# Two units' queries, and two units' keys, in one transfer each, with the keys' odd chunks in front

## The chip, the cores and the metric

One core of a Trainium2 chip runs the whole program. The metric is the device time of one execution in microseconds (us); a kernel's figure is the median over its runs. The core has five engines with an instruction queue each: TensorE (PE, matmuls; its weight loads are listed as PEld), VectorE (DVE), ScalarE (ACT), GpSimd (POOL) and SyncE (SP), which here only issues DMA transfers and waits for semaphores. Each queue runs in order.

## The reference, cut to what matters

```
scores = 0.125 * q @ k^T                      # 4 batches, 8 heads, 576 positions, 64 wide
heads 0..3: a query sees itself and the 31 keys before it
heads 4..7: a query sees keys at distance 0, 4, 8, ... below 128
attn = softmax(scores);  x = attn @ v         # x: 2304 tokens x 512
logits = x @ phi                              # soft mixture of experts, 8 experts x 4 slots
slot_input = softmax over tokens(logits)^T @ x
slot_out[e] = relu(slot_input[e] @ w1[e]) @ w2[e]
x = softmax over slots(logits) @ slot_out
h = x @ w_in;  g = max(h, 0) + alpha * min(h, 0);  out = g @ w_out
```

All arrays are float32. For heads 4 to 7 the host sorts positions by their remainder modulo 4, so that a dilated window becomes a plain one of 32.

## The kernel before

**Units and groups.** A unit u (16 of them) is one batch and two heads; with head width 64 its q and k fill 128 partitions, 576 columns each. A unit is cut into 9 blocks of 64 queries, and 8 consecutive blocks over the units make a group g (18 of them), so a group touches one or two units. Per group PE preloads the mask (`sm`, L254), computes the scores (`s`, L263: 16 matmuls of 64 keys), later transposes the probabilities (`t`, L298) and multiplies with v (`pv`, L311). DVE and ACT do the softmax between them (`max`, `sub`, `exp`, `sum`, `rec`), POOL the normalising, ACT the copies out of PSUM (`te`, and half of `ev`). Between the groups PE also computes the router's logits (`lt`), transposes of x (`x`) and the slot sums (`part`).

**How q, k and v come in.** For each unit SP issues one transfer for q, one for k (`load_qk`, L240, 288 KB each, 2304 bytes a partition) and one for v (`load_v`, L248, 576 KB, 4608 bytes a partition). q lands in a raw buffer: that of units 2 and 3 lies in `xs_m`, all others use two in `q_m` in turn. ACT and DVE then copy it, one head each (`emit_qx`, tasks `qx`), into one of four slots with zeros between the heads. k has four slots of 32 + 576 columns (the 32 are zeros, for the block before the first), v has four. So q of unit u waits for the `qx` of unit u - 2, k for the last `s` of unit u - 4, `qx` for that too, v for the last `pv` of unit u - 4.

**The expert weights** come in 32 transfers of 1024 KB (8192 bytes a partition, L185) on the same SP queue, in the order of use. Twelve have buffers of their own, which are free from the start; nine go into the memory of q, k, v, the probabilities and xs when attention has left it; the last eleven reuse buffers as experts consume them. Then follow the first 1024 KB transfers of the last layer (`w_f`, L183).

**The order** on every engine in the attention part is made at build time by a planner (`schedule`): a list of tasks with their needs, a due time (`k - 20` for q and k) and a cost of occupation and latency (`COST`). It takes the task that could start first; SP is one of its engines ("dma"), and a weight transfer is what it takes when nothing of attention may start. The chip then runs each engine's queue in that order and waits on semaphores.

**After attention** come the slot sums, then the experts (`emit_l1` L596, `emit_hT` L609, `emit_l2` L618) with some matmuls without use (`warm`, L407) around the last expert, then the conversion of the first `w_f` (`conv`, L668 to L678) and the last layer, which takes the rest of the time and doesn't touch q, k or v.

## Time and profile before

| what | us |
|---|---|
| median of 3 runs (387.76 to 390.1) | 389.87 |
| the profiled execution | 390.64 |
| its span, first to last instruction | 388.9 |
| PE busy in the span | 364.7 |
| attention, up to the first expert matmul | 97.3 |
| experts, up to the last L618 | 141.5 |
| the last layer | the rest |

The profiled execution is 1.7 us longer than its span, and 0.8 us above the median. 75.19 MB move in all, most of it in the first 150 us; over the whole span that is 193 GB/s. A profile says busy time by engine, but the three stages have different limits, so each is read from its own stretch.

### The profile page before, as it was taken

The numbers are of one execution on the slowest core, as the hardware profiler recorded it, in microseconds if no ns is written. First come the engines' busy times: TensorE is split into PE (matmuls) and PEld (weight loads), VectorE is DVE, ScalarE is ACT, GpSimd is POOL, SyncE is SP. The second block draws the span as 40 slices with busy tenths as digits, with TensorE's granted clock in tenths as the row PEclk, the third lists the DMA queues.
The fourth block names the chain that finished last, engine by engine and source line by source line (L and its number), as shares of the span: only waits on it lengthen the run. The fifth ranks groups of instructions, "written<-read, shape, count | busy, mean of one in ns | idle before, by whom it ended". The sixth has DMA issues, their size and how long they took to land.

```text
span 388.9 us, 7912 instructions
## 1 busy us (share of the span) xinstructions
PE 364.7 (94%) x3126; PEld 272.1 (70%) x3126; DVE 262.3 (67%) x454; ACT 218.2 (56%) x467; POOL 142.4 (37%) x125
## 2 busy tenths in 40 slices
PE   7689899998999688899999999999999999999995
PEld 4477687865444256577877787887788878778884
DVE  5888889765166139989999998939974324234363
ACT  2478778664232028877766746656754645446460
POOL 4223222220000004446456556545564444444460
PEclk9999999999999899989999999999999999999998
DMA  8999999999999995053332325100000000001336
GB/s 294 393 353 360 397 397 407 408 418 422 420 419 421 420 421 201 10 207 109 109 110 108 108 110 163 55 0 0 3 1 0 2 0 1 2 0 56 108 128 197
DMA packets 17173, 75.19 MB, mean 193 GB/s; under 512 B 2128, under 2 KB 2528, under 8 KB 10992
## 3 DMA queue, kind: packets, MB, share of 16 engines
q1 hardware_dynamic: 16160, 72.98, 48.9%
q10 hardware_dynamic: 912, 1.64, 1.2%
q8 instruction: 24, 0.39, 0.4%
q14 instruction: 13, 0.11, 0.1%
q0 software_dynamic: 64, 0.07, 0.1%
HBM read 69.97 MB, written 4.72 MB: 192 GB/s over the span
## 4 chain that ended last, share of the span: by engine, by line
PE 50%; DVE 22%; DMA 16%; ACT 6%; issue 3%; POOL 1%; SPq 1%; DVEq 0%; POOLq 0%; ACTq 0%
PE y L802 32%; DMA w<-w 9%; DMA q_m<-qk 7%; DVE gs L796 5%; PE pv L311 3%; DVE wo_lo L685 3%; PE hb L788 2%; PE si L391 2%; DVE pt_m L675 2%; PE x L382 2%; DVE pt_m L678 2%; PE s L263 2%; DVE e_m L672 2%; DVE e_m L675 2%; DVE e_m L670 1%
## 5 line engine op out<-in xcount | busy, mean ns | idle before, releaser
L896 POOL TENSOR_TENSOR gls<-gs,ghs 128x384 fp32r<-128x384 f32 x96 | 117.6, 1241 | 170.4 <-ACT ghs L327 142.0
L802 PE MATMUL y<-wo_hi,ghs 128*128 128x512 f32 x289 | 97.6, 401 | 0.8 <-ACT ghs L327 0.4
L796 DVE SCALAR_TENSOR_TENSOR gs<-gs,beta_s,hb 128x384 f32<-128x384 f32 x96 | 56.5, 609 | 51.6 <-ACT gs L890 49.2
L802 PE MATMUL y<-wo_lo,ghs 128*128 128x512 f32 x289 | 89.3, 394 | 0.0
L802 PE MATMUL y<-wo_hi,gls 128*128 128x512 f32 x289 | 86.2, 394 | 2.3 <-POOL gls L896 2.3
L890 ACT ACTIVATE gs<-hb 128x384 f32<-128x384 f32 x96 | 44.9, 492 | 36.8 <-PE hb L788 31.4
L327 ACT CAST ghs<-gs 128x384 fp32r<-128x384 f32 x96 | 49.4, 517 | 28.0 <-DVE gs L796 27.5
L802 PEld LDWEIGHTS y<-wo_hi,gls 128*128 128x128 f32 x289 | 54.4, 189 | 14.3 <-POOL gls L896 3.6
L802 PEld LDWEIGHTS y<-wo_hi,ghs 128*128 128x128 f32 x289 | 53.7, 189 | 14.9 <-issue 1.8
L802 PEld LDWEIGHTS y<-wo_lo,ghs 128*128 128x128 f32 x289 | 54.4, 189 | 10.7 <-issue 0.2
L293 POOL TENSOR_TENSOR e_m<-e_m,l 128x512 f32<-128x512 f32 x18 | 19.1, 1062 | 58.9 <-DVE l L289 36.4
L788 PE MATMUL hb<-cpack,mpack 128*128 128x384 f32 x96 | 31.5, 346 | 1.4 <-DVE mpack L782 0.8
L263 PEld LDWEIGHTS s<-q_m 128*64 128x64 f32 x576 | 18.7, 138 | 7.5 <-issue 4.5
L311 PE MATMUL pv<-pt_m,v_m 128*64 128x64 f32 x576 | 20.0, 224 | 2.8 <-ACT pt_m L327 2.7
L311 PEld LDWEIGHTS pv<-pt_m,v_m 128*64 128x64 f32 x576 | 18.1, 138 | 6.3 <-ACT pt_m L327 3.8
L263 PE MATMUL s<-q_m 128*64 128x64 f32 x576 | 21.2, 225 | 1.1 <-ACT q_m L327 1.0
L788 PEld LDWEIGHTS hb<-cpack,mpack 128*128 128x128 f32 x96 | 17.8, 188 | 5.7 <-DVE mpack L782 1.5
L327 ACT COPY pt_m<-t 64x512 f32<-64x512 f32 x36 | 20.8, 579 | 0.9 <-PE t L298 0.2
L670 DVE TENSOR_SCALAR pt_m<-pt_m 128x1024 f32<-128x1024 f32 (+1 forms) x9 | 8.1, 900 | 18.9 <-ACT pt_m L668 18.9
L599 ACT ACTIVATE v_m<-h,rinv 128x256 f32<-128x256 f32 x8 | 3.8, 474 | 20.8 <-PE h L596 16.2
L329 DVE COPY xt<-pv 128x256 f32<-128x256 f32 (+7 forms) x32 | 9.5, 306 | 8.7 <-ACT xt L327 8.5
L618 PE MATMUL o<-w,hT 128*32 128x512 f32 x88 | 12.5, 640 | 3.1 <-DMA w<-w 3.1
(157 smaller groups left out, 492.6 us busy)
## 6 DMA issues: line engine op xcount, KB each, us to landing
w<-w SPq DMA_DIRECT2D x23, 1024.0 KB, 12.8
v_m<-v SPq DMA_DIRECT2D x16, 576.0 KB, 7.0
q_m<-qk SPq DMA_DIRECT2D x30, 288.0 KB, 6.0
q_m<-w_f SPq DMA_DIRECT2D x8, 1024.0 KB, 5.0
v_m<-w_f SPq DMA_DIRECT2D x7, 1024.0 KB, 4.8
q_m<-w SPq DMA_DIRECT2D x4, 1024.0 KB, 17.7
v_m<-w SPq DMA_DIRECT2D x2, 1024.0 KB, 16.7
e_m<-w SPq DMA_DIRECT2D x1, 1024.0 KB, 15.0
```

What stands on the lines that cost most here:

```text
L263: mm(s[r:r + 64, col:col + 64], lhsT=q_of(u)[:, 2 * o:2 * o + 64], rhs=k_of(u)[:, o:o + 64], start=False, stop=True, skip_group_check=True)
L293: nc.gpsimd.tensor_tensor(out=e, in0=e, in1=bc(e_[g, "l"], 128, 8, 64), op=ALU.mult)
L311: mm(pv[hs, n], lhsT=vv[u % 4][:, c, hs], rhs=pts[:, NBS * (g % 2) + n, h], start=True, stop=True, skip_group_check=True)
L327: nc.scalar.copy(out=out, in_=in_)
L618: mm(o[32 * g:32 * g + 32, :], lhsT=ht[:, 4 * r + g, 28 - 4 * e:60 - 4 * e], rhs=w[:, g, :], start=(e == 0 and r == 0), stop=(e == NE - 1 ...
L670: nc.vector.tensor_scalar(out=t, in0=t, scalar1=2.0 ** -15, scalar2=FMAX, op0=ALU.max, op1=ALU.min)
L675: nc.vector.scalar_tensor_tensor(out=ti, in0=w[:, 1::2], scalar=-0x40000000, in1=ti, op0=ALU.bitwise_and, op1=ALU.bitwise_or)
L788: mm(hb[i], lhsT=mpack[:, 128 * f:128 * f + 128], rhs=cpack[:, t0:t0 + 384], start=True, stop=True)
L796: nc.vector.scalar_tensor_tensor(out=g, in0=g, scalar=beta_s[:, f:f + 1], in1=hb[i], op0=ALU.mult, op1=ALU.add)
L802: mm(y[steps[s][0], t][:, sl], lhsT=g, rhs=wo_hl[p == 1][:, f, sl], start=start, stop=stop, skip_group_check=True)
L890: lambda s=s, i=i: nc.scalar.activation(out=half(gs, s, i, 4), in_=hb[i], func=AF.Relu, scale=-1.0),
L896: lambda s=s, i=i: nc.gpsimd.tensor_tensor(out=half(gls, s, i, 6), in0=half(gs, s, i, 4), in1=half(ghs, s, i, 6).bitcast(F32), op=ALU.subt ...
```

## The change

Units are taken in pairs. For units 0 and 1 q and k come as before, one transfer per unit and array. For the 14 other units one transfer brings both units' q (576 KB, 4608 bytes a partition) and one both units' k. The raw q of a pair lies in `xs_m` for units 2 and 3, and in one buffer in `q_m` for all others. k has two slots of pairs, with one stretch of 32 zeros in front of each instead of one per unit. The order of a unit's 18 chunks of 32 keys is changed on the host: the nine odd ones first, then the nine even ones. The 64 keys of a score matmul are then two runs of 32 columns, 288 or 320 columns apart, and for the second half of a block the odd chunk comes first; mask and v (built on the host) follow that order. The number of matmuls, copies and softmax instructions stays.

A pair's q now waits for the `qx` of both units of the pair before it (for units 4 and 5: of 0 and 1), its k for the last `s` of both units two pairs before. The planner makes a new order of all attention tasks from that and from the new costs. The diff also has a way to copy parts of v on POOL (`COPIED`), which is empty here and makes no instruction. The one-element constant of ones becomes a column, set before the first matmul instead of later.

```
-            q=(0.75, 2.9), k=(0.75, 2.9), ...
+            q=(0.75, 2.9), k=(0.75, 2.9), qq=(1.45, 3.6), ...
+COPIED = ()
-KZ = S + WIN
+KP = 2 * S + WIN
...
-            j = 64 * c + kj - 32 * (1 - x)
+            j = 64 * c + (kj + 32) % 64 if x else 64 * c + kj - 32
...
+    def k_pair(p):
+        return part(q_m[:, NQ * QZ:], p % 2, KP)
+
+    def keys(u, c, x):
+
+        a, n = NQ * QZ + KP * (u // 2 % 2) + S * (u % 2) + 32 * (c + x), S // 2 + 32 * (1 - x)
+        return q_m[:, a:a + 2 * n].rearrange("p (b k) -> p b k", b=2)[:, :, 0:32]
+
+    def q_pair(p):
+        return xs_m[:, 0:2 * S] if p == 1 else q_m[:, NQ * QZ + 2 * KP:][:, 0:2 * S]
+
     def q_raw(u):
-        return part(xs_m, u - 2, S) if u in (2, 3) else part(q_m[:, NQ * (QZ + KZ):], u % 2, S)
+        return part(q_pair(u // 2), u % 2, S)

-    def load_qk(u, x):
-        nc.sync.dma_start(out=k_of(u)[:, WIN:] if x else q_raw(u), in_=qk[u, :, x])
+    def load_qk(p, x, c0=0, c1=2 * S):
+        nc.sync.dma_start(out=(k_pair(p)[:, WIN:] if x else q_pair(p))[:, c0:c1], in_=qk[p, :, x, c0:c1])
...
-                    mm(s[r:r + 64, col:col + 64], lhsT=q_of(u)[:, 2 * o:2 * o + 64], rhs=k_of(u)[:, o:o + 64],
+                    mm(s[r:r + 64, col:col + 64], lhsT=q_of(u)[:, 2 * o:2 * o + 64], rhs=keys(u, c, x),
...
+                p, odd = divmod(u, 2)
+                if first[u] == g and p == 0:
+                    task(("q", u), "dma", lambda u=u: load_qk(0, 0, S * u, S * u + S), [], k - 20)
+                    task(("k", u), "dma", lambda u=u: load_qk(0, 1, S * u, S * u + S), [], k - 20)
+                elif first[u] == g and not odd:
+                    task(("q", u), "dma", lambda p=p: load_qk(p, 0), [("qx", w, h) for w in {1: (), 2: (0, 1)}.get(p, (u - 2, u - 1)) for h in range(2)],
+                         k - 20, "qq")
+                    task(("k", u), "dma", lambda p=p: load_qk(p, 1), [("s", last[u + 1 - NQ])] if u >= NQ else [], k - 20, "qq")
                 if first[u] == g:
-                    task(("q", u), "dma", lambda u=u: load_qk(u, 0), [("qx", {4: 0, 5: 1}.get(u, u - 2), h) for h in range(2) if u > 3], k - 20)
-                    task(("k", u), "dma", lambda u=u: load_qk(u, 1), [("s", last[u - NQ])] if u >= NQ else [], k - 20)
...
+        nc.vector.memset(ones_s, 1.0)
         zero = pt_m[:, 0:512]
...
+        for i in range(2):
+            nc.vector.memset(k_pair(i)[:, 0:WIN], 0.0)
         for i in range(NQ):
-            nc.vector.memset(k_of(i)[:, 0:WIN], 0.0)
...
-        nc.vector.memset(one_s, 1.0)
```

SP's queue, from the first transfer after units 0 and 1 to the first expert weight. `xs_m` and `q_m` from `qk` are q or k, `v_m` is v, `w` an expert weight; the number at the end of a row is a repeat. Before:

```order
L240 DMA xs_m<-qk 128x576
L240 DMA q_m<-qk 128x576
L248 DMA v_m<-v 128x1152
L240 DMA xs_m<-qk 128x576
L240 DMA q_m<-qk 128x576
L248 DMA v_m<-v 128x1152
L240 DMA q_m<-qk 128x576 x2
L248 DMA v_m<-v 128x1152
L240 DMA q_m<-qk 128x576 x2
L248 DMA v_m<-v 128x1152
L240 DMA q_m<-qk 128x576 x4
L185 DMA w_80<-w 128x2048
```

The same stretch of the change, and two pairs further:

```order
L250 DMA xs_m<-qk 128x1152
L250 DMA q_m<-qk 128x1152
L259 DMA v_m<-v 128x1152 x2
L250 DMA q_m<-qk 128x1152 x2
L259 DMA v_m<-v 128x1152 x2
L187 DMA w_80<-w 128x2048
L250 DMA q_m<-qk 128x1152 x2
L259 DMA v_m<-v 128x1152
L187 DMA w_81<-w 128x2048
L259 DMA v_m<-v 128x1152
L250 DMA q_m<-qk 128x1152
```

The first weight now stands in front of q and k of units 6 and 7, where it stood behind them; the second stands in front of those of units 8 and 9.

PE's queue around the scores of group 6, which are the first to need unit 6 (the third `s` row from here on is group 7's; `t`, `pv` and `lt` are named above). Before:

```order
L298 MATMUL t<-eye_s,e_m 128x128 x4
L254 LDWEIGHTS m_m
L254 MATMUL s<-m_m 128x512
L263 MATMUL s<-q_m 64x64 x16
L341 MATMUL lt<-xt_116,phi_s 32x192 x3
L298 MATMUL t<-eye_s,e_m 128x128 x4
L311 MATMUL pv<-pt_m,v_m 64x64 x16
L254 LDWEIGHTS m_m
L254 MATMUL s<-m_m 128x512
L263 MATMUL s<-q_m 64x64 x16
L311 MATMUL pv<-pt_m,v_m 64x64 x16
```

The same stretch of the change:

```order
L317 MATMUL t<-eye_s,e_m 128x128 x4
L273 LDWEIGHTS m_m
L273 MATMUL s<-m_m 128x512
L360 MATMUL lt<-xt_116,phi_s 32x192 x3
L317 MATMUL t<-eye_s,e_m 128x128 x4
L330 MATMUL pv<-pt_m,v_m 64x64 x16
L282 MATMUL s<-q_m 64x64 x16
L317 MATMUL t<-eye_s,e_m 128x128 x4
L273 LDWEIGHTS m_m
L273 MATMUL s<-m_m 128x512
L330 MATMUL pv<-pt_m,v_m 64x64 x16
L282 MATMUL s<-q_m 64x64 x16
```

The scores of group 6 moved behind the logits, the transposes of group 3 and the `pv` of group 2, and one more group's transposes come before the scores of group 7.

## Rows read from the trace of the kernel before

**Rows 1.** The page's 40 slices: DMA busy in tenths, and GB/s.

```profile
DMA  8999999999999995053332325100000000001336
GB/s 294 393 353 360 397 397 407 408 418 422 420 419 421 420 421 201 10 207 109 109 110 108 108 110 163 55 0 0 3 1 0 2 0 1 2 0 56 108 128 197
```

**Rows 2.** Windows (stretch, length, busy by engine, clock, DMA share, GB/s).

```profile
5.00:10.00 5.00, 3.65 (x68) 2.33 (x66) 3.06 (x9) 3.02 (x4) 0.29 (x1) 1.00 1.04 398
10.00:15.00 5.00, 3.32 (x67) 2.56 (x68) 4.69 (x11) 2.05 (x4) 1.04 (x1) 1.00 1.05 402
...
25.00:30.00 5.00, 4.49 (x103) 3.38 (x100) 4.25 (x10) 4.56 (x9) 0.00 (x0) 1.00 0.93 322
...
120.00:125.00 5.00, 4.91 (x60) 2.22 (x59) 3.33 (x7) 1.82 (x5) 0.00 (x0) 1.00 1.01 418
```

**Rows 3.** Chain of waits, experts (start, us, what ran or was waited for).

```profile
97.33 1.09 PE h L596 x16
...
98.45 14.03 DMA w<-w
...
112.54 21.38 DMA w<-w
...
133.96 1.84 PE o L618 x8
135.79 2.38 PE st L407 x12
...
139.17 1.31 PE st L407 x10
140.48 1.04 PE o L618 x8
...
142.03 0.67 ACT pt_m L668
```

**Rows 4.** PE's timeline, last experts (start, us; idle before, and who ended it).

```profile
127.53 1.91 PE L596 MATMUL h<-w,slotT 128*32 128x256 f32 x32
131.56 1.07 PE L618 MATMUL o<-w,hT 128*32 128x512 f32 x8 [2.12 <-DMA w<-w]
132.55 0.44 PE L609 MATMUL t<-eye_s,v_m 128*128 128x128 f32 x2
133.96 1.84 PE L618 MATMUL o<-w,hT 128*32 128x512 f32 x8 [0.97 <-DMA w<-w]
```

**Rows 5.** SP's timeline: a steady stretch of 1024 KB transfers.

```profile
119.99 0.33 SPq L183 DMA_DIRECT2D q_m<-w_f  x1
122.48 0.33 SPq L183 DMA_DIRECT2D xs_m<-w_f  x1
```

**Rows 6.** Windows around the experts' end (clock is the third number from the right).

```profile
129.40:134.00 4.60, 1.51 (x18) 0.43 (x17) 0.00 (x0) 0.66 (x2) 0.00 (x0) 1.00 1.01 420
134.00:137.50 3.50, 3.50 (x16) 1.89 (x17) 0.00 (x0) 0.00 (x0) 0.00 (x0) 0.52 1.00 419
```

**Rows 7.** The page's DMA issues: KB each, median us from issue to landing.

```profile
v_m<-v SPq DMA_DIRECT2D x16, 576.0 KB, 7.0
q_m<-qk SPq DMA_DIRECT2D x30, 288.0 KB, 6.0
```

**Rows 8.** Chain of waits, first 41 us: landings of q that ACT waited for.

```profile
10.31 9.50 DMA q_m<-qk
...
19.89 0.67 ACT q_m L327
20.56 0.53 ACT e_m L280
...
35.33 5.04 DMA q_m<-qk
```

**Rows 9.** SP's timeline, where it waits for a copy of q.

```profile
12.44 0.33 SPq L248 DMA_DIRECT2D v_m<-v  x1
17.70 3.21 SPq L240 DMA_DIRECT2D q_m<-qk  x4
```

**Rows 10.** PE's timeline, groups 6 and 9.

```profile
24.40 1.15 PE L263 MATMUL s<-q_m 128*64 128x64 f32 x32
25.48 0.53 PE L341 MATMUL lt<-xt,phi_s 128*32 128x192 f32 x6
25.94 0.65 PE L298 MATMUL t<-eye_s,e_m 128*128 128x128 f32 x4
26.70 1.15 PE L311 MATMUL pv<-pt_m,v_m 128*64 128x64 f32 x32
...
35.70 1.15 PE L263 MATMUL s<-q_m 128*64 128x64 f32 x32
```

**Rows 11.** DVE's timeline: the zeros in front of k.

```profile
1.36 0.09 DVE L504 MEMSET q_m<- 128x32 f32 x1
```

More of the change, by code (lines that the diff above doesn't have):

```diff
@@ L159, in tile_kernel @@
     beta_s = const.tile([128, DFF // 128], F32, name="beta_s")
[L160 removed]
+    ones_s = const.tile([128, 1], F32, name="ones_s")
+    one_s = ones_s[0:1]
     slotT = keep.tile([128, 4, NS], F32, name="slotT")
@@ L247, in load_v, with emit_vc @@
     def load_v(u):
-        nc.sync.dma_start(out=part(v_m, u % 4, 128 * NC), in_=v[u])
+        r = slice(32, 96) if u in COPIED else slice(0, 128)
+        nc.sync.dma_start(out=part(v_m, u % 4, 128 * NC)[r], in_=v[u, r])
+    def emit_vc(u, x, i):
+        w = part(v_m, u % 4, 128 * NC)
+        r, o, d = ((64, 0, 128), (32, 96, 0))[i]
+        a, b = 128 * (0, 5)[x] + d * (x == 0), 128 * (5, NC)[x]
+        nc.gpsimd.tensor_tensor(out=w[o:o + 32, a:b], in0=w[r:r + 32, a - d:b - d],
+                                in1=ones_s[r:r + 32].to_broadcast([32, b - a]), op=ALU.mult)
     def emit_sm(g):
@@ L426, in tasks_of_attention @@
                         task(("qx", u, h), eng, lambda u=u, h=h, e=eng: emit_qx(u, h, e),
-                             [("q", u)] + ([("s", last[u - NQ])] if u >= NQ else []), k - 5.0, "qx%d" % h)
-                    task(("v", u), "dma", lambda u=u: load_v(u), [("pv", last[u - 4])] if u >= 4 else [], k - 8)
+                             [("q", u if p == 0 else 2 * p)] + ([("s", last[u - NQ])] if u >= NQ else []), k - 5.0, "qx%d" % h)
+                    task(("v", u), "dma", lambda u=u: load_v(u), [("pv", last[u - 4])] if u >= 4 else [], k - 8 - 3 * (u in COPIED),
+                         "vh" if u in COPIED else "v")
+                    for n in range(4 * (u in COPIED)):
+                        task(("vc", u, *divmod(n, 2)), "pool", lambda u=u, n=n: emit_vc(u, *divmod(n, 2)), [("v", u)], k + 4.5 + 2.5 * (n > 1))
             task(("sm", g), "pe", lambda g=g: emit_sm(g), [("sub", g - 2)], k - 2.6)
-            task(("s", g), "pe", lambda g=g: emit_s(g), [(n, u, *h) for u in units for n, h in (("k", ()), ("qx", (0,)), ("qx", (1,)))] + [("sm", g)],
+            task(("s", g), "pe", lambda g=g: emit_s(g),
+                 [("k", u if u < 2 else u - u % 2) for u in units] + [("qx", u, h) for u in units for h in range(2)] + [("sm", g)],
                  k - 2.5)
@@ L441, in tasks_of_attention @@
             ev = [("ev", f, u, x) for f in (g - 2,) for u in sorted({w for _, w, _ in blocks(max(f, 0))}) for x in range(2)]
-            task(("pv", g), "pe", lambda g=g: emit_pv(g), [("te", g, x) for x in range(2)] + ev + [("v", u) for u in units], k + 8.0)
+            task(("pv", g), "pe", lambda g=g: emit_pv(g), [("te", g, x) for x in range(2)] + ev + [("v", u) for u in units]
+                 + [("vc", u, int(c > 4), i) for _, u, c in blocks(g) for i in range(2)], k + 8.0)
             for u in units:
@@ L502, in tile_kernel @@
         nc.scalar.dma_start(out=m_m[:, 320:64 + 64 * (NST + 2)].bitcast(BF16), in_=mask[:, 640:])
+        for i in range(2):
+            nc.vector.memset(k_pair(i)[:, 0:WIN], 0.0)
         for i in range(NQ):
-            nc.vector.memset(k_of(i)[:, 0:WIN], 0.0)
             (nc.vector if i < 2 else nc.gpsimd).memset(q_of(i), 0.0)
+        for i in sorted({u % 4 for u in COPIED if u < 4}):
+            nc.gpsimd.memset(part(v_m, i, 128 * NC)[0:32, 0:128], 0.0)
         nc.vector.tensor_copy(out=eye_s, in_=eye16_s)
@@ L919, in pairs_t, with odd_first @@
     def pairs_t(a):
-        return perm(a).transpose(0, 1, 3, 2).reshape(NU, 2 * D, 1, S)
+        return perm(a).transpose(0, 1, 3, 2).reshape(NU // 2, 2, 2 * D, S)
+    def odd_first(a):
+        a = a.reshape(*a.shape[:3], NC, 2, 32)
+        return np.concatenate([a[:, :, :, :, 1], a[:, :, :, :, 0]], axis=3)
     def halves_of(w):
@@ L930, in features @@
         return np.concatenate([i.reshape(NF, 128, DM), o], axis=2)
-    pv = np.pad(perm(v), ((0, 0), (0, 0), (WIN, 0), (0, 0)))
-    halves = [pv[:, :, o:o + S].reshape(B, HP, 2, NC, 64, D).transpose(0, 1, 4, 3, 2, 5) for o in (0, WIN)]
-    vp = np.stack(halves, axis=2).reshape(NU, 128, NC * 2 * D)
+    vp = np.pad(perm(v), ((0, 0), (0, 0), (WIN, 0), (0, 0))).reshape(B * HP, 2, -1, 32, D)
+    vp = np.stack([vp[:, :, i:i + 2 * NC - 1:2] for i in (0, 1, 2, 1)], axis=1)
+    vp = vp.transpose(0, 1, 4, 3, 2, 5).reshape(NU, 128, NC * 2 * D)
+    qk = np.stack([pairs_t(q), odd_first(pairs_t(k)).reshape(NU // 2, 2, 2 * D, S)]).transpose(1, 3, 0, 2, 4).reshape(NU // 2, 2 * D, 2, 2 * S)
     arrays = {
-        "qk": np.concatenate([pairs_t(q), pairs_t(k)], axis=2), "v": vp, "phi": moe_phi.reshape(HP, 128, NS).transpose(1, 0, 2), "w1": halves_of(moe_w1), "w2": halves_of(moe_w2),
+        "qk": qk, "v": vp, "phi": moe_phi.reshape(HP, 128, NS).transpose(1, 0, 2), "w1": halves_of(moe_w1), "w2": halves_of(moe_w2),
         "w_f": features(moe2_w_in, moe2_w_out),
```

7 lines of the change are left out of this document (2 added, 5 removed).

## Prediction

> **What bounds the kernel now.** I read the page's slices first. The DMA engines are full for the first 15 slices, some 146 us, at 294 to 422 GB/s, and then fall away [rows 1]. So up to the end of the experts the transfers may be the limit; behind that they are not, and nothing that this change touches is used there. The windows say how full and how fast: from 5 us on the DMA share is about 1, at 398 and 402 GB/s while mostly q and k (2304 bytes a partition) and v (4608) move, at 418 while only weights (8192) move; one early window sinks to 322 with a share of 0.93 [rows 2]. The reader should see a queue that hardly ever runs dry, and a rate that depends on what is in it.
>
> Next comes the chain of waits, to see whether a full queue also sets the end. It does: after the first expert matmul at 97.33 the chain goes over two transfers, from 98.45 to 112.48 and from 112.54 to 133.92, and only then back to PE [rows 3]. The long times from issue to landing are time in the queue: in the steady stretch SP issues one transfer of 1024 KB each time an older one lands, 122.48 - 119.99 = 2.49 us apart [rows 5].
>
> PE's timeline shows how much PE would gain without that. It runs without a gap until 127.53 + 1.91 = 129.44, waits 2.12 us for one weight and 0.97 us for the next [rows 4], 3.09 us in all. In that stretch it is busy for 1.51 of 4.6 us, and right behind it the granted clock is 0.52, which is the 1.2 GHz level [rows 6]. That costs more: the 8 instructions of L618 take 1.84 instead of 1.07 us [rows 4], and the 12 of L407 take 2.38, where 10 take 1.31 at full clock [rows 3], so 1.57 for 12. Together 0.77 + 0.81 = 1.58 us. If weights were always there in time, the experts would end 3.09 + 1.58 = 4.67 us earlier. That is the most that any faster stream can give. It is also the other way round a cushion: attention may end up to 4.7 us later before the experts end later than now.
>
> **The change part by part.** (1) Fewer, longer rows. 28 transfers of 288 KB become 14 of 576 KB. The bytes stay: 28 x 294,912 B = 8.26 MB. At 400 GB/s, the mean of the two full windows with such rows [rows 2], they take 20.6 us; at 418 GB/s 19.8 us. The stream gets 0.9 us shorter. Bounds: nothing, if the lower rate has another cause than the rows; and 8.26 MB at 322 GB/s are 25.6 us, so 5.9 us, if the sunken window were due to the rows, of which 4.67 can reach the end. I take 0.9, since the 322 stand beside a share of 0.93 [rows 2], and a queue that runs low is no matter of row length. All weights stand behind q, k and v in the same queue, so the last weight comes 0.9 us earlier, if the queue doesn't run dry in a new place.
>
> The Trainium skill has two rules on this term. "SBUF — State Buffer", section "The DMA setup-cost knee", says that every transfer pays about 2 us whatever its size, and advises to coalesce; with 14 transfers fewer that would be an estimated 28 us. The trace disagrees for this queue: transfers of 1024 KB that take 14 and 21 us from issue to landing [rows 3] land 2.49 us apart [rows 5], so what is fixed lies beside other transfers. "Perfetto Trace Analysis", section "DMA Optimizations", says against this change that smaller chunks let some work start sooner; part (2) is what that would mean here.
>
> (2) Later first use. Unit 6 is the place to look at. Now q of units 6 and 7 stands ahead of the first weight on SP; in the change behind it, as the two lists of SP's queue show. Counted from a landing that the chain shows: q of unit 5 lands at 10.31 + 9.50 = 19.81 [rows 8], by the order of before after q of units 0 to 5, k of 0 to 4 and v of 0 to 2. The change moves, up to the pair q of 6 and 7, three units' worth of q and k more (3 x 0.74 us at 400 GB/s), one v (1.47) and one weight (2.49): 6.2 us, so 26.0. k of the pair follows 1.4 us later, at 27.4. The scores of group 6 ran at 24.40 [rows 10], so they come 3.0 us later. But PE's list has changed as well: the logits, the transposes and the `pv` that stood behind them now stand ahead, and these ended at 26.70 + 1.15 = 27.85 with the scores (1.15) before them [rows 10], so at 26.7 without. PE loses 27.4 - 26.7 = 0.7 us. For units 8 and 9 in the same way: a weight, v of 4, 5 and 6, q and k come after 27.4, that is 2.49 + 5 x 1.45 = 9.7 us (1.45 between 1.41 and 1.47), so 37.1, and group 9 needs them, whose scores ran at 35.70 [rows 10]: 1.4 us later. The two are not added in full, since a delay of group 6 also moves what stands before group 9; I take 1.5 us for the end of attention, with 0 and 4.7 as the bounds within the cushion.
>
> (3) New waits on SP. The pair q of 6 and 7 waits for the copies of q of units 4 and 5, not of 4 alone. SP already stands from 12.44 to 17.70 for such a copy [rows 9]; the copy for unit 5 starts at 19.89 [rows 8], some 2 us behind. Behind it in SP's queue are k of the pair, v of 4 and a weight. What covers the wait is what is queued already: the first weight alone is 2.49 us. If that cover is gone, the stream stands still for as long, and the 0.9 are lost. k of units 4 and 5 also waits for group 2 instead of group 1, with two v and three pairs issued ahead of it as its cover.
>
> (4) What costs nothing: two zeroings of 0.09 us less on DVE [rows 11], and the column of ones ahead of PE's first matmul, all of it while the first q is still on its way: the first zeroing runs at 1.36 us [rows 11], and a q takes 6.0 us in the median from issue to landing [rows 7]. If that cover were gone, it would be a gain of some 0.1 us. PE has as many matmuls as before.
>
> **The sum.** Stream: -0.9 us. Attention 1.5 us later: inside the cushion. PE is then ready for the waited weight at 129.44 + 1.5 = 130.9, which comes at 131.56 - 0.9 = 130.7 [rows 4]: the wait of 2.12 us is gone, and of the second, 133.96 - 0.9 = 133.1 against 130.9 + 1.43 = 132.4, 0.7 us are left. If with so little idle time the clock stays at 2.4 GHz, the last L618 waits for the last weight alone: two transfers behind 133.92, so 133.92 + 2 x 2.49 - 0.9 = 138.0 instead of 140.48 [rows 3]. The conversion after it (ACT, 142.03 [rows 3]) needs the first `w_f`, one more transfer later, 140.5. So the gain would be 142.03 - 140.5 = 1.5 us; with the clock falling as now it is 0.9. I take 1.2. The profiled execution has 390.64 us, 0.8 above the median of the runs, 389.87; the forecast goes from the median: 388.7.
>
> **The rivals.** Nothing comes through: the rate in rows 2 is not due to the rows, or SP's new waits eat the 0.9. Against it: the share stays near 1 at 400 and at 418 GB/s [rows 2], so the engines, not the queue, are slower with the short rows. 389.9 us.
>
> Slower: each pair pays on SP what units 6 to 9 pay. There are two slots of pairs for k and one buffer for the raw q of most pairs, SP's queue is in order, and v and weights stand behind each wait. If each of the 6 pairs from units 4 and 5 on cost PE between the 1.4 us of group 9 and the 3.0 us by which group 6's keys are late, attention ends 8.4 to 18 us later; the cushion takes 4.7 of that, and it decides from there. Middle, 6 x 2.2 = 13.2, so 8.5 us: 398.4; the low end is 393.6. For it: ACT waits for q already now, 5.04 us of the chain at 35.33 alone [rows 8]. Against it: from about 40 us on the DMA engines are full at about 400 GB/s and more in every slice [rows 1], though some of these waits are there already.
>
> The two runs of keys. If PE read 2 x 32 columns at half the speed of 64 in a row, each group's 1.15 us [rows 10] would double; 18 x 1.15 = 20.7, less the cushion 16: 406 us. No row shows a moving operand in two runs. The Trainium skill's "Advanced Engine Details and Errata", section "Memory Cachelines", says that any non-contiguous access pattern significantly slows matmuls, but of PSUM; for SBUF it asks for two hits on a line of 16 bytes. No run here shows it; the operand here is in SBUF.
>
> The full cushion: the low rates between 20 and 40 us are the short rows after all, and the stream gets over 3.9 us shorter. Then PE sets the experts' end: 389.9 - 4.7 = 385.2 us.
>
> **Chances.** Forecast (stream shorter, attention inside the cushion) 0.62; nothing comes through 0.15; SP's waits 0.13; two runs of keys 0.04; full cushion 0.06. About 1%, 3.9 us, is what a measurement of this kernel can tell from no change. Faster by more is the last case and the upper end of the first: 0.07. Slower by more is the two runs of keys and most of SP's waits: 0.14. Within: 0.79. The forecast's own range is 387.4 (all of 1.5, and 1 us more from the sunken window) to 389.9. The range to hold 8 in 10 goes to 386.2, part of the way into the full cushion, and to 392.6, to where attention uses up the cushion and 2.7 us more; the rest of SP's waits, the slow keys and the full cushion are left out.
>
> **What would show it.** Right: in the windows from 5 to 15 us the rate rises from 400 towards 418; the waits of L618 for weights shrink from 3.09; the clock stays at 1.00 around 134 to 137; the conversion starts at about 140.5 to 141.1; the `s` groups keep 1.15 us. Wrong: a DMA share well below 1 before 45 us, a first expert matmul after 102 us (97.33 + 4.7), or ACT and PE waiting for q and k after 45 us.

## The result, and the profile after

The change takes 385.28 us in the median of 13 runs (383.44 to 388.28), the kernel before 389.05 (386.98 to 391.59) beside it: ratio 0.9919, interval 0.9897 to 0.9941. That is 3.8 us faster, where 1.2 was forecast, and 0.9 us below the range's lower end of 386.2; it is still within 1%. Of the distance to the forecast 0.8 us is the starting point: the forecast went from 389.87, the median of three runs, and thirteen give 389.05. Two later timings of the unaltered change gave 386.64 (0.9948, 0.9915 to 0.9981) and 386.90 (0.9939, 0.9907 to 0.9971), both inside the forecast's range. The mean of the three ratios, 0.9935, is 2.5 us. The runs of nearly every kernel spread over 3 us and more, and those of the change follow the granted clock (last section), so one profile says little about 1 us.

The profiled execution of the change took 387.63 us, span 385.9; that of before 390.64 and 388.9. Windows of the change (columns as in [rows 2]):

```profile
5.00:10.00 5.00, 4.65 (x69) 2.59 (x67) 2.84 (x7) 2.20 (x3) 0.29 (x1) 1.00 1.04 407
10.00:15.00 5.00, 3.16 (x66) 2.33 (x66) 4.84 (x11) 2.41 (x4) 0.74 (x1) 1.00 1.02 410
...
25.00:30.00 5.00, 4.88 (x100) 3.77 (x94) 3.96 (x10) 3.99 (x8) 1.21 (x2) 1.00 0.86 305
...
15.00:60.00 45.00, 41.58 (x770) 33.37 (x771) 35.31 (x87) 31.92 (x71) 12.24 (x12) 0.92 0.98 391
60.00:65.00 5.00, 5.00 (x81) 3.03 (x81) 4.87 (x11) 4.04 (x8) 1.28 (x2) 1.00 0.83 302
60.00:90.00 30.00, 29.38 (x539) 21.80 (x539) 22.47 (x58) 21.55 (x50) 7.53 (x9) 1.00 0.98 393
134.00:137.50 3.50, 3.50 (x30) 1.73 (x28) 0.00 (x0) 0.18 (x1) 0.00 (x0) 1.00 1.00 419
```

The same three longer windows of before:

```profile
15.00:60.00 45.00, 40.87 (x795) 31.97 (x796) 37.13 (x92) 33.62 (x72) 11.78 (x11) 1.00 1.00 377
60.00:65.00 5.00, 5.00 (x98) 4.02 (x95) 4.27 (x13) 3.58 (x11) 1.45 (x2) 1.00 1.02 408
60.00:90.00 30.00, 29.08 (x540) 22.19 (x539) 21.48 (x56) 20.88 (x51) 7.18 (x8) 1.00 1.02 415
```

The reader should see a gain and a loss: 391 instead of 377 GB/s from 15 to 60 us, (391 - 377) x 45 us = 0.63 MB more, and 393 instead of 415 from 60 to 90 us, 0.66 MB less, most of it in the five microseconds at 302. By 90 us this execution has moved no more than before; its twelfth weight lands at 87.8 us, before at 87.7.

PE's timeline of the change answers [rows 4]; its first row is the first expert matmul, 97.33 in [rows 3]:

```profile
99.14 4.48 PE L629 MATMUL h<-w,slotT 128*32 128x256 f32 x48 [0.20 <-DVE slotT L598]
...
131.04 1.91 PE L629 MATMUL h<-w,slotT 128*32 128x256 f32 x32
132.77 1.04 PE L651 MATMUL o<-w,hT 128*32 128x512 f32 x8
133.74 0.44 PE L642 MATMUL t<-eye_s,v_m 128*128 128x128 f32 x2
134.11 1.06 PE L651 MATMUL o<-w,hT 128*32 128x512 f32 x8
```

Attention ended 1.8 us later and PE no longer waits for weights: the 2.12 and 0.97 us are gone. The chain of waits answers [rows 3]:

```profile
137.70 1.31 PE st L426 x10
139.02 1.04 PE o L651 x8
140.56 0.68 ACT pt_m L701
```

The conversion starts at 140.56 instead of 142.03, 1.47 us earlier. It follows the last L651, which ends at 140.06; the first `w_f` had landed at 139.94. The rest takes 385.9 - 140.56 = 245.3 instead of 388.9 - 142.03 = 246.9 us, 1.5 less, though nothing was changed there. What SP's timeline shows of the weights in the first 50 us, before:

```profile
20.96 0.43 SPq L185 DMA_DIRECT2D w<-w  x1
...
30.93 0.58 SPq L185 DMA_DIRECT2D w<-w  x1
...
36.18 0.42 SPq L185 DMA_DIRECT2D w<-w  x1
...
45.31 0.43 SPq L185 DMA_DIRECT2D w<-w  x1
```

And in the change:

```profile
12.37 0.43 SPq L187 DMA_DIRECT2D w<-w  x1
...
25.03 0.76 SPq L187 DMA_DIRECT2D w<-w  x1
...
31.75 0.43 SPq L187 DMA_DIRECT2D w<-w  x1
...
37.37 0.43 SPq L187 DMA_DIRECT2D w<-w  x1
...
43.75 0.91 SPq L187 DMA_DIRECT2D w<-w  x2
```

Six weights are issued by 45 us instead of three. The first goes out before SP stands waiting for a copy of q (until 19.06 us), not behind that wait.

### The profile page after: what moved, and what is told of

It reads as the page before. It is cut to its first block, busy times and chain, and to the rows that moved or that the text cites. A ratio compares the mean times of both kernels' runs of the same rounds, so it can differ in the third digit from the quotient of the medians.

```text
span 385.9 us, 7887 instructions
## 1 busy us (share of the span) xinstructions
PE 366.5 (95%) x3126; PEld 273.7 (71%) x3126; DVE 261.9 (68%) x452; ACT 217.2 (56%) x467; POOL 144.0 (37%) x125
## 2 busy tenths in 40 slices
DMA packets 15156, 75.19 MB, mean 195 GB/s; under 512 B 1904, under 2 KB 2304, under 8 KB 8976
## 4 chain that ended last, share of the span: by engine, by line
PE 57%; DVE 24%; DMA 7%; ACT 5%; issue 4%; POOL 1%; SPq 0%; DVEq 0%; ACTq 0%; POOLq 0%
PE y L835 31%; DMA q_m<-qk 6%; DVE gs L829 5%; PE h L629 4%; PE o L651 4%; PE pv L330 3%; PE hb L821 2%; DVE wo_lo L718 2%; PE s L282 2%; DVE e_m L705 2%; DVE pt_m L711 2%; DVE e_m L708 2%; PE si L410 2%; PE x L401 2%; DVE e_m L703 1%
## 5 line engine op out<-in xcount | busy, mean ns | idle before, releaser
L835 PE MATMUL y<-wo_hi,ghs 128*128 128x512 f32 x289 | 96.6, 398 | 1.0 <-ACT ghs L346 0.7
L282 PEld LDWEIGHTS s<-q_m 128*64 128x64 f32 x576 | 19.5, 145 | 4.8 <-issue 2.4
L330 PEld LDWEIGHTS pv<-pt_m,v_m 128*64 128x64 f32 x576 | 19.0, 143 | 4.8 <-ACT pt_m L346 2.6
L330 PE MATMUL pv<-pt_m,v_m 128*64 128x64 f32 x576 | 21.0, 229 | 0.3
L346 ACT COPY xt<-pv 128x256 f32<-128x256 f32 (+7 forms) x32 | 8.7, 279 | 10.8 <-DVE xt L348 6.5
```

Source lines behind the costliest of these rows:

```text
L282: mm(s[r:r + 64, col:col + 64], lhsT=q_of(u)[:, 2 * o:2 * o + 64], rhs=keys(u, c, x), start=False, stop=True, skip_group_check=True)
L330: mm(pv[hs, n], lhsT=vv[u % 4][:, c, hs], rhs=pts[:, NBS * (g % 2) + n, h], start=True, stop=True, skip_group_check=True)
L346: nc.scalar.copy(out=out, in_=in_)
L835: mm(y[steps[s][0], t][:, sl], lhsT=g, rhs=wo_hl[p == 1][:, f, sl], start=start, stop=stop, skip_group_check=True)
```

## The experiments

Theories at the start: **rows** (longer rows move faster, the forecast's reason) against the new order, and **clock** (PE no longer waits, so the clock no longer falls). From e5 on the theory of the order is **fill** (it puts weights, which wait for nothing, in front of transfers that wait, so more is under way while SP stands). Each row of the table is one kernel: its time, then readings of its one profiled execution. "Twelfth" and "last" are the landings of those expert weights, "rest" is the span less the conversion's start.

| kernel | median us | ratio, interval | GB/s 15-60 / 60-90 | first expert matmul | twelfth / last | conversion | rest |
|---|---|---|---|---|---|---|---|
| before | 389.05 | | 377 / 415 | 97.3 | 87.7 / 138.9 | 142.0 | 246.9 |
| before, second profile (e12) | | | 383 / 416 | 96.3 | 86.6 / 137.1 | 140.2 | 246.9 |
| change | 385.28 | 0.9919, 0.9897-0.9941 | 391 / 393 | 99.1 | 87.8 / 137.5 | 140.6 | 245.3 |
| change (e1) | 386.64 | 0.9948, 0.9915-0.9981 | 398 / 375 | 99.9 | 88.0 / 137.7 | 141.3 | 245.1 |
| change (e13) | 386.90 | 0.9939, 0.9907-0.9971 | 395 / 392 | 98.8 | 86.5 / 136.6 | 139.1 | 246.6 |
| split pairs (e2) | 385.18 | 0.9906, 0.9868-0.9944 | 408 / 404 | 96.4 | 84.7 / 134.5 | 137.0 | 246.0 |
| one transfer more (e3) | 386.68 | 0.9958, 0.9922-0.9995 | 407 / 398 | 97.0 | 85.5 / 136.6 | 139.2 | 245.3 |
| before, warm (e4) | 388.43 | 0.9993, 0.9964-1.0021 | 379 / 418 | 96.3 | 86.8 / 137.8 | 140.3 | 245.2 |
| before, new SP order (e5) | 385.99 | 0.9943, 0.9917-0.9968 | 408 / 409 | 99.3 | 84.9 / 134.6 | 139.0 | 247.0 |
| change, weights late (e6) | 392.50 | 1.0091, 1.0058-1.0124 | 354 / 416 | 96.5 | 89.2 / 140.0 | 142.5 | 245.4 |
| before, weights early (e7) | 386.25 | 0.9934, 0.9907-0.9960 | 395 / 403 | 96.9 | 86.3 / 136.0 | 138.5 | 245.9 |
| change, plain keys (e8) | 386.14 | 0.9942, 0.9911-0.9973 | 406 / 388 | 98.2 | 86.8 / 136.5 | 139.6 | 245.3 |
| before, weights earlier (e9) | 389.36 | 1.0032, 0.9995-1.0068 | 387 / 377 | 98.4 | 89.7 / 139.4 | 141.9 | 245.8 |
| split, weights earlier (e10) | 387.11 | 0.9961, 0.9932-0.9990 | 406 / 412 | 99.6 | 84.9 / 134.5 | 139.3 | 246.7 |
| change, early warm (e11) | 387.75 | 0.9978, 0.9952-1.0003 | 396 / 383 | 98.9 | 87.9 / 137.6 | 140.2 | 245.2 |

e1 to e4 ran beside each other, as did e5 to e8, e9 and e10, and e11 to e13; the medians of before beside them were 388.54, 388.59, 388.19 and 388.82.

**The change again.** No edit.

> The change once more, unaltered, so that the next kernels stand beside it on one chip. Theory A (the wait for weights): the shorter stream takes away PE's 3.1 us of waiting for the last expert weights and the clock level that fell behind it; the gain up to the first conversion is 1.5 us in the profile. Theory B (clock chance): the part beyond 1.5 us comes from stretches at 1.2 GHz that fall at different places in every execution. Both expect 385.3 us, 3 to 4 us less than before; by B the times of single executions follow their mean granted clock.

386.64. The gain stands: 0.52% (0.19 to 0.85), beside 0.81% the first time.

**Pairs split.** The two halves of each pair transfer on their own, 288 KB with rows of 2304 bytes, everything else as in the change:

```diff
-        nc.sync.dma_start(out=(k_pair(p)[:, WIN:] if x else q_pair(p))[:, c0:c1], in_=qk[p, :, x, c0:c1])
+        for c in range(c0, c1, S):
+            nc.sync.dma_start(out=(k_pair(p)[:, WIN:] if x else q_pair(p))[:, c:c + S], in_=qk[p, :, x, c:c + S])
```

> The change with each pair's transfer issued as two of 288 KB with rows of 2304 bytes again, one directly behind the other; the planner's order, the slots of pairs and the layout of the keys stay as in the change. If the longer rows and fewer transfers are the gain (my sum's 0.9 us of stream), the last expert weight lands 0.9 us later than in the change and the time goes back by 0.9 to 1.5 us, to 386.2 to 386.8 us. If the new order is the gain, the time stays at that of the change, 385.3 us.

385.18, 0.9906. The rows are as short as before, and the gain is all there: as its cause **rows** has fallen. Its windows:

```profile
5.00:10.00 5.00, 4.55 (x72) 2.79 (x70) 3.27 (x8) 2.91 (x5) 0.29 (x1) 1.00 1.04 392
10.00:15.00 5.00, 3.04 (x68) 2.43 (x68) 4.80 (x13) 1.69 (x4) 1.04 (x1) 1.00 1.04 404
...
15.00:60.00 45.00, 41.65 (x814) 32.96 (x815) 37.17 (x89) 34.02 (x75) 12.22 (x11) 1.00 1.03 408
60.00:65.00 5.00, 5.00 (x112) 3.60 (x107) 3.58 (x10) 3.66 (x7) 1.04 (x1) 1.00 0.98 350
```

From 15 us on this stream is as full as any, with short rows. (408 - 377) x 45 us is 1.40 MB more by 60 us, less (415 - 404) x 30 us = 0.33 MB until 90 us: 1.07 MB, 2.5 us at 419 GB/s. The twelfth weight lands 3.0 us earlier. The first two windows show what the rows do give, beside 407 and 410 in the change: from 5 to 10 us all seven profiles with pairs in one transfer run at 402 to 408 GB/s, the eight others at 391 to 399. So the longer rows did move faster, by some 3%, and the times don't show it. Whether the length of a row or the size of a transfer does it isn't parted here.

**One transfer more.** The change with one further transfer of 576 KB that nothing reads, ahead of the 22nd weight:

```diff
+        if i == 21:
+            nc.sync.dma_start(out=m_m[:, 64:64 + 2 * S], in_=qk[1, :, 0, 0:2 * S])
```

> The change with one more transfer of 576 KB (a copy of q that nothing reads) in front of the expert weight that first reuses a buffer, so that the last weights land 1.4 us later, about as late as before. Theory A: PE waits for the last weights again, and the time goes back by 1.4 us or more, to 386.7 to 389 us. If the stream is not what sets the experts' end in the change, the time stays at 385.3 us.

386.68, the median of the change beside it. Its profile has a wait of 1.03 us for the last weight again, but its attention ended 2.9 us earlier than that of e1. The time doesn't tell the theories apart.

**Warm matmuls in the kernel before.** Seven and three matmuls without use where PE waits for the weights of the last expert but one:

```diff
+            if e == NE - 2:
+                wm = ps_c.tile([128, 512], F32, tag="c", name="wm")
+                warm(7, wm[:, 0:128])
...
+            if e == NE - 2:
+                warm(3, wm[:, 0:128])
```

> The kernel before with 7 and 3 of its matmuls without use where PE waits 2.1 and 1.0 us for the weights of the last but one expert; transfers as before. If the clock level that falls behind that wait is a part of the gain, PE stays at 2.4 GHz there and the experts end about 0.6 us earlier (the conversion is then bound by its own transfer, which lands at 141.4 us against 142.0), and the last layer can gain too: 386.5 to 388.5 us against 389.0. If the clock there plays no part, the time stays at 389.0 us or gets longer by what the matmuls delay the weights' use, up to 0.5 us.

388.43, no change, although the 1.2 GHz stretch at 134 us was gone from its profile (its stretches begin at 96.7 and 144.5). By this run the **clock** behind that wait is no part of the gain.

**The kernel before with the change's order on SP.** Slots, rows, keys and copies as before; SP must take the transfers in the change's order, each pair's two transfers one behind the other (here up to the fifth weight; numbers of q, k and v are units):

```diff
+SP_ORDER = q0 k0 q1 k1 q2 q3 k2 k3 v0 v1 q4 q5 k4 k5 v2 v3 w0 q6 q7 k6 k7 v4 w1 v5 q8 q9 v6 k8 k9 w2 v7 k10 k11 w3 q10 q11 v8 v9 w4 ...
-            if any(x not in end_at for x in need):
+            if any(x not in end_at for x in need) or engine == "dma" and name != sp[0]:
```

> The kernel before (single slots for k, raw q of single units, rows of 2304 bytes, keys in a row), with SP's queue in the order that the change has: q of two units, then k of two, and the expert weights between them at the change's places; the planner arranges the other engines around it. Theory F (fill): the change gains because the weights, which wait for nothing, stand further forward in SP's queue, so that more bytes are under way while SP waits for a copy of q; then this kernel gains all of it: about 385.5 us against 388.5, and in the profile the rate between 15 and 40 us is about 400 GB/s as in e2_split, with the last expert weight at 134 to 136 us. Theory S (slots and layout): it is the pairs' slots or the keys' layout; then this stays at 388.5 us.

385.99, 0.9943: the gain without any of the change's transfers. The stream is that of the split run:

```profile
15.00:60.00 45.00, 42.04 (x839) 33.63 (x840) 37.35 (x91) 34.30 (x75) 12.00 (x11) 1.00 1.03 408
```

**The change with the weights late.** The change, pairs and long rows and all, with the weights at about the places that they had before:

```diff
-  ... v2 v3 w0 q6 k6 v4 w1 v5 q8 v6 k8 w2 v7 k10 w3 q10 ...
+  ... v2 v3 q6 k6 w0 v4 v5 q8 v6 k8 w1 v7 k10 q10 w2 v8 v9 q12 k12 w3 ...
```

> The change with its pairs, rows of 4608 bytes and layout, but with the expert weights at the places that they have in the kernel before: the first behind q and k of units 6 and 7, the second behind those of 8 and 9, and so on. Theory F: less is under way when SP waits, the rate between 15 and 40 us falls below 390 GB/s, the last expert weight lands at 138 us or later, and the time is 387.5 to 389.5 us. Theory R (rows of 4608 bytes): the gain stays, 385.3 to 386.6 us.

392.50, 1.0091. With long rows, and slower than before. Its window, and PE's timeline at the last weights:

```profile
15.00:60.00 45.00, 42.72 (x871) 34.55 (x872) 40.02 (x97) 34.36 (x76) 13.27 (x13) 1.00 0.92 354
```

```profile
130.04 1.07 PE L635 MATMUL h<-w,slotT 128*32 128x256 f32 x16 [2.31 <-DMA w<-w]
132.62 1.93 PE L657 MATMUL o<-w,hT 128*32 128x512 f32 x8 [1.52 <-DMA w<-w]
```

The queue runs dry (share 0.92) and PE waits 3.83 us for two weights. This is about what the change would have been without the moved weights.

**The kernel before with its weights early.** On SP only the first seven weights move, each to about where the weight ahead of it stood: the first ahead of q and k of unit 6 instead of behind those of 7.

```diff
-  ... v3 q6 k6 k7 q7 w0 v4 q8 k8 q9 v5 k9 k10 v6 w1 ...
+  ... v3 w0 q6 k6 k7 q7 w1 v4 q8 k8 q9 w2 v5 k9 k10 v6 q10 k11 w3 ...
```

> The kernel before with one thing moved: the first seven expert weights one place each further forward on SP (the first in front of q of unit 6 instead of behind q of unit 7, and so on); q, k and v keep their order, slots and rows. Theory F: a good part of the gain comes from this alone, 385.5 to 387.5 us. If q must come in pairs for the gain, the time stays at 388.5 us.

386.25, 0.9934. So the place of the weights alone, with what the planner makes of it, is worth as much as the change. Its window:

```profile
15.00:60.00 45.00, 41.97 (x803) 33.04 (x803) 37.12 (x89) 33.34 (x70) 11.47 (x11) 0.96 1.01 395
```

One rival has no run of its own: in e5, e6 and e7 the planner also made new orders for PE, ACT and DVE, to suit the order given to SP. Against it speaks the end of attention. The first expert matmul comes at 99.3 and 96.9 us in e5 and e7, which gain, and at 96.5 in e6, which loses, beside 97.3 and 96.3 before: attention wasn't shorter where the kernel gained.

**Keys in their own order.** The change with the 64 keys of a score matmul in one run again, mask and v to match:

```diff
-        a, n = NQ * QZ + KP * (u // 2 % 2) + S * (u % 2) + 32 * (c + x), S // 2 + 32 * (1 - x)
-        return q_m[:, a:a + 2 * n].rearrange("p (b k) -> p b k", b=2)[:, :, 0:32]
+        a = NQ * QZ + KP * (u // 2 % 2) + S * (u % 2) + 64 * c + 32 * x
+        return q_m[:, a:a + 64]
```

> The change with the keys in their natural order, so that the 64 keys of a score matmul stand in a row again; mask and v follow. All else, SP's order too, is as in the change. My prediction: two runs of 32 columns cost nothing, the groups of scores take 1.15 us either way and the time is that of the change, 385.3 to 386.6 us. If two runs cost something, this is faster by it.

386.14, beside 385.28 to 386.90 of the change. The groups of score matmuls (count, busy us, mean ns of one), before, change, split pairs (two runs of keys as well) and plain keys:

```profile
L263 PE MATMUL s<-q_m 128*64 128x64 f32 x576 | 21.2, 225 | 1.1 <-ACT q_m L327 1.0
```

```profile
L282 PE MATMUL s<-q_m 128*64 128x64 f32 x576 | 21.7, 232 | 1.8 <-DVE l L307 1.4 <-ACT q_m L346 0.3
```

```profile
L283 PE MATMUL s<-q_m 128*64 128x64 f32 x576 | 20.8, 224 | 2.0 <-DVE l L308 1.5
```

```profile
L282 PE MATMUL s<-q_m 128*64 128x64 f32 x576 | 20.7, 224 | 2.9 <-DVE l L303 1.7 <-DMA q_m<-qk 0.7 <-ACT pt_m L346 0.4
```

The change's row has 1.0 us more than that of plain keys, but in its profile PE stood at 1.2 GHz from 17.5 to 24.3 us, among the scores. The split run and e8 have no such stretch before 98 us, and there two runs of 32 columns take as long as one of 64, 224 ns. They cost no time that the runs show either.

**Weights one place further still.** Each weight of the kernel before one more place forward than in e7, the first ahead of q of unit 4 (`w0 q4 k4 v2 q5 k5 v3 w1 q6 ...`), and the same on the split form (`w0 q4 k4 v2 v3 w1 q6 k6 v4 w2 ...`).

> The kernel before, with all expert weights further forward on SP: one place more than where the run with seven weights moved had them, so the first weight stands ahead of q and k of unit 4. Theory 'fill' (what counts is how many bytes are under way while SP waits for copies of q): the windows between 15 and 30 us, 349 to 407 GB/s there, stay at 390 or more, the last weight lands at 134 to 136 us, L618 waits for weights under 0.8 us in all; but PE then sets the end of the experts, 40.6 us behind the first expert matmul (from 96.43 to 137.00 in the split run), so at best 385 to 386, no clear gain over 386.25. Rival 'later units': the weights in front make units 4 to 7 late, the first expert matmul goes beyond 100 us and the time to 387 or more. Rival 'stream only': every place further forward gives the same again, 384 or less.

> The change with its pair transfers split in two (288 KB each) and every expert weight one place further forward on SP than in the change, the first one ahead of q and k of units 4 and 5. Theory 'fill': in the split run no L618 waited for a weight any more, so PE sets the end of the experts and more fill brings nothing: 384.5 to 386, last weight before 134.5 us, conversion about 40.6 us behind the first expert matmul. Rival 'later units': q and k of units 4 to 7 come about 2.5 us later, ACT and PE wait, first expert matmul beyond 99 us, 387 or more. Rival 'stream only': another 2 us less, 383.

389.36 and 387.11. In the kernel before that is too far: 1.0032 (0.9995 to 1.0068), where e7 gave 0.9934. The split form keeps a gain, 0.9961 (0.9932 to 0.9990), and its interval overlaps that of e2 (0.9868 to 0.9944). There the stream gains nothing more (the last weight at 134.52 instead of 134.48), and attention ends 3.2 us later. In the kernel before the rate falls again at 75 to 80 us, to 314 GB/s. That only twelve weights are free from the start, so that those spent early are missing there, is argued, not shown.

**Early matmuls, and both kernels once more.** The change with 18 matmuls without use in PE's first waits:

```diff
+        if g == 0:
+            warm(8, t[:, 0:128])
...
+            if (g, m) == (4, 2):
+                t_[1] = ps_t.tile([128, 512], F32, tag="t", name="t")
+                warm(10, t_[1][:, 0:128])
```

> The change, with 18 matmuls without use on PE in two early waits: 8 ahead of the first group's transposes (wait of 1.23 us at about 14 us) and 10 in the middle of group 4's scores (wait of 1.44 to 1.90 us at about 17 us). In two profiled executions of the change the granted clock fell to 1.2 GHz at 17.5 and 18.2 us, right behind these waits, and the DMA rate of 15 to 40 us was 371 and 384 GB/s; in four kernels with the same place of the weights and no such fall it was 402 to 407. Theory 'the early clock fall gives part of the fill back' (attention late, SP waits for its copies): no 1.2 GHz stretch before 40 us, 400 GB/s or more from 15 to 40 us, twelfth weight at 85 to 86 us instead of 87.8 to 88.0, time 1 us under the change unaltered in this call. Rival 'the clock there is hidden': the fall goes away and the time stays within 0.5 us of the change unaltered. Rival 'no cure': the clock falls all the same, no difference.

> The change, unaltered, beside the run with early matmuls. Theory 'the early clock fall is a matter of chance in the change too': the profile may lack the fall at 17 to 18 us; without it the rate from 15 to 40 us is 400 GB/s or more and the twelfth weight lands at 85 to 86.5 us; with it 370 to 385 and 87.5 to 88. Rival 'it belongs to the change': the fall is there a third time. The time: 385.2 to 386.7, the two medians so far.

387.75 against 386.90. The clock stayed at 1.00 from 15 to 40 us, but the rate there was 381 GB/s, and the twelfth weight landed at 87.94. That doesn't settle the theory, since the matmuls without use held PE up themselves: the second half of group 4's scores, behind them, began no earlier than with the clock's fall (18.28 in the change, 18.54 in e13). SP's next v, which waits for a `pv`, goes out at 23.27 us in e11, 24.65 in the change and 21.86 in e8. PE's timeline of e11, and of e8, which has the change's orders and no fall there:

```profile
19.61 0.69 PE L285 MATMUL s<-q_m 128*64 128x64 f32 x16
```

```profile
18.20 0.69 PE L282 MATMUL s<-q_m 128*64 128x64 f32 x16 [1.69 <-DVE l L303]
```

From 15 to 40 us the three profiles of the change, all with the fall, show 371, 384 and 382 GB/s, and e8 and e3, with the same orders and no fall at 17 us, 404 and 402. So the record speaks for the theory as far as the rate goes; the times show no difference (386.14 and 386.68 beside 385.28 to 386.90). Windows of e11:

```profile
15.00:60.00 45.00, 42.19 (x800) 34.21 (x800) 36.09 (x87) 32.32 (x72) 12.03 (x12) 1.00 1.01 396
60.00:65.00 5.00, 5.00 (x84) 3.03 (x84) 4.85 (x11) 3.99 (x8) 1.21 (x2) 1.00 0.76 262
```

The sunken window at 60 us is there again, as in all six profiles with the change's order and pairs in one transfer (302, 271, 299, 331, 312 and 262 GB/s), and less deep in the two with that order and halves (350 in e2, 362 in e5). SP's timeline of the change and of the split run shows what goes ahead of it:

```profile
54.92 0.43 SPq L187 DMA_DIRECT2D w<-w  x1
61.88 0.80 SPq L250 DMA_DIRECT2D q_m<-qk  x2
```

```profile
52.59 0.43 SPq L187 DMA_DIRECT2D w<-w  x1
58.02 2.87 SPq L251 DMA_DIRECT2D q_m<-qk  x4
```

Behind a weight SP stands until the raw q of the pair before has been copied: 6.5 us in the change (6.2 to 7.2 in the six profiles), 5.0 in the split run. That the first copies can start sooner with halves is argued, not shown.

> The kernel before, unaltered, for a second profile. In its first one the transfer that lands at 131.42 us comes 4.04 us behind the one ahead of it instead of 2.48, and so makes the last four weights 1.56 us late; the run with warm matmuls added to it and the change with late weights show the like at 132.85 (3.85) and 129.99 (3.54), the others only behind the weights, at 147 to 150 us, or nowhere. Theory 'part of the kernel before': a step of 3.5 to 4.1 us again between 127 and 135 us. Rival 'a chance event of each execution': it is elsewhere or missing, and L618 waits for weights 1.5 us or less in all.

Its PE timeline at the last weights:

```profile
129.80 1.07 PE L618 MATMUL o<-w,hT 128*32 128x512 f32 x8 [1.42 <-DMA w<-w]
...
132.19 1.93 PE L618 MATMUL o<-w,hT 128*32 128x512 f32 x8 [0.96 <-DMA w<-w]
```

The late transfer of the first profile is not there (one of 3.29 us lies at 89.90 instead): it is an event of single executions. The waits for weights belong to the kernel before, 2.38 us in all here, 3.09 in [rows 4].

## Why the prediction was wrong, point by point

In short: the step that failed is (1), with (2) beside it. The sum's gain began with 0.9 us of stream from longer rows, and it counted the moved weights as a delay and as cover for new waits only. The runs show the order on SP in its place: short rows kept the gain (e2, 0.9906), the order without pairs gave it (e5, 0.9943; e7, 0.9934), and pairs with the weights late lost it (e6, 1.0091). The sum also put nothing behind the conversion, where the profiles of the change are 1.2 us shorter in the mean (246.9 to 245.7); the cause of that is open.

**What bounds it: right.** The experts waited for the stream: in both profiles of before, and in e3, e6, e7, e9 and e11, PE stands for weights near the end.

**Step (1), rows: half right on the rate, wrong as the cause of the gain.** The step put 400 against 418 GB/s down to row length and set the sunken window of 322 aside, since "a queue that runs low is no matter of row length". The second half of that sentence was true, and the conclusion wrong: time lay in the sunken windows, and the kernels that gained filled them by another road (391 to 408 GB/s from 15 to 60 us, 377 and 383 before). Halving the rows again kept the gain (e2), keeping the rows long with the weights late lost it (e6). The change's 5 to 15 us reached 407 and 410, not 418; e2 with short rows has 392 and 404 there, so 0.2 us ((408 - 398) x 10 us = 0.1 MB) are what the pair transfers themselves give in that stretch. If the difference held for all 8.26 MB, it would be an estimated 0.5 us (20.7 at 398 GB/s, 20.2 at 408), where the step had 0.9.

**Step (2), the weight ahead of units 6 and 7: only its cost was seen.** The step priced the move of a weight as 2.49 us of delay for q and k, and step (3) saw in it a cover for the change's new wait. Neither asked what the weight gains against the kernel before, where nothing stood ahead of that wait. Moving weights alone gave 0.66% (e7), moving them back cost more than it had given (e6). The times settle that the order on SP does it, the weights' place above all. That it acts by filling the queue is argued from the rates: 354 to 383 GB/s from 15 to 60 us in all four profiles with the weights at the old places, 387 to 408 in all eleven others. The rate doesn't order the times by itself: e9 has 387 and no gain, and the change has given its lead back by 90 us.

**The cushion: right in kind, its size in part chance.** The first expert matmul came at 99.14, 1.8 us later (1.5 forecast; the mean of the change's three profiles is 99.3, of the two before 96.8, so 2.5). In that execution PE also lost 4.48 - 2.80 = 1.68 us in its first 48 expert matmuls (2.80 is what they take in e2 and e7), where the granted clock fell at 99.5. With the 1.47 that the conversion gained this makes 5.0 us, and that is the cushion's size by the traces: from the first expert matmul to the last of the experts 44.2 us before (97.33 to 141.52), 39.2 in e2 (96.43 to 135.61), where 4.67 was forecast. The conversion at 140.56 hit the forecast's 140.5 by luck. The forecast had it wait for the first `w_f`, and it waited for PE; the two other profiles of the change have 141.3 and 139.1. And 1.56 of the 3.09 us of waits in [rows 4] came from one late transfer of that execution: the first waited weight landed at 131.42, 4.04 us behind the one ahead of it, where 2.48 is usual. The profile of before was taken at its word; e12 gives 2.38 us.

**Step (3), SP's waits: partly wrong.** The cover of the first pair wait held only in part in the change's three profiles, all with PE at 1.2 GHz from 17.5 or 18.2 us on: from 20 to 25 us they have 352, 339 and 342 GB/s, where e8 and e3, with the same orders and no such stretch there, have 392 and 405. The 305 GB/s at a share of 0.86 from 25 to 30 us stand in the first profile alone (387 and 383 in e1 and e13). The window from 20 to 25 us of e1, and of e8:

```profile
20.00:25.00 5.00, 5.00 (x108) 3.99 (x106) 3.76 (x9) 2.95 (x8) 2.27 (x2) 0.84 0.96 339
```

```profile
20.00:25.00 5.00, 4.88 (x119) 3.95 (x116) 4.08 (x11) 3.40 (x9) 1.53 (x2) 1.00 1.01 392
```

At 55 to 62 us the cover is gone in all six profiles, and from 60 to 65 the change's share is 0.83: 0.66 MB are lost from 60 to 90 us, 1.6 us at 419 GB/s. That is the stand of the stream that step (3) named, and it may be why the change gains less than its own order could: e2 has the twelfth weight 3.1 us ahead of the change's. By the times that isn't shown: e2 and e1 can't be told apart (385.18 and 386.64, the intervals overlap).

The Trainium skill's "Perfetto Trace Analysis", section "DMA Optimizations", says that smaller chunks may let some work start sooner, and the trace agrees as far as SP's wait goes: 5.0 us with halves, 6.5 without. The other rule named ahead, "SBUF — State Buffer", section "The DMA setup-cost knee" of the Trainium skill, would make e2, with 14 transfers more than the change, an estimated 28 us slower; the run disagrees, e2 is no slower.

**Step (4) and the two runs of keys: right.** No price shows (224 ns for a score matmul in e2 and in e8).

**The sum and the rivals.** Of the signs named, the waits of L618 went away, the clock stayed at 1.00 from 134 to 137 us, the conversion came at 140.56, the `s` groups kept their time at full clock. Of the signs against, a share well below 1 before 45 us came (0.86 from 25 to 30 us in the change's first profile, 0.95 to 0.96 from 20 to 25 in the two others), and the kernel gained all the same. ACT's waits for q after 45 us did not grow (2.6 us, 2.9 before). The full cushion at 385.2 us had a chance of 0.06. The first median is there, the two later ones are 1.4 and 1.6 us above it; PE does set the experts' end, as that rival had it. Its reason, that the low rates early on "are the short rows after all", was its error: the order did it, and no rival said so.

**What stays open.** How the 2.5 us split. Over the profiles the span falls from 388.0 (mean of two) to 386.0 (of three): 0.8 us up to the conversion (141.1 to 140.3) and 1.2 behind it (246.9 to 245.7). Nor do the profiles show a lead of the change's own stream at its end: the last weight lands at 137.5, 137.7 and 136.6, before at 138.9 and 137.1, of which the 138.9 holds the late transfer. Such a lead shows in e2, e5 and e7 (134.5 to 136.0). So that the change itself gains by the stream is argued from these and from e6. Behind the conversion nothing was changed. There the granted clock tells the two values apart; the window from 161.5 to 168.2 us, before and change:

```profile
161.50:168.20 6.70, 5.03 (x14) 3.50 (x14) 6.70 (x8) 4.71 (x10) 5.57 (x4) 0.75 0.46 157
```

```profile
161.50:168.20 6.70, 5.62 (x30) 3.99 (x31) 6.70 (x7) 5.83 (x13) 6.18 (x4) 1.00 0.44 157
```

Five of the fifteen profiles (before twice, e5, e10, e13) have a 1.2 GHz stretch that begins between 161 and 165 us and a rest of 246.6 to 247.0; the ten others have none there but one that begins between 139 and 147 us, about where PE waits for the conversion anyway, and a rest of 245.1 to 246.0. (e5 and e10 have both.) Whether a kernel that doesn't wait for weights falls more often into the cheaper case isn't settled: e4 fell into it in its profile and kept its median.

## What to carry to other kernels

When an in-order queue issues both transfers that wait for a buffer and transfers that wait for nothing, put one of the second kind ahead of each long wait: here that was worth 0.66%, and pairs with the weights back cost 0.9%; one place further in the kernel before, and the gain was gone (1.0032). Read a sunken rate window as a question about what was queued at that time, not as noise beside the full windows, and look for it in a second profile before resting on it. When a planner makes the order, compare its queue before and after first: a change of shapes may act through the order alone.
